# Early score masks by ScalarE and GpSimd, r loads from ScalarE's queue, and a denser start of the weight conversion, in a fused RWKV-7 and feed-forward kernel

## Chip, cores and metric

One core of one Trainium2 chip. The metric is device time in microseconds (us), the median over several executions of one program. All timed runs quoted here are of the fast state unless a line says otherwise. Profile times are counted from the start of the profiled execution. PE is TensorE's matmul side and PEld its weight loads, DVE is VectorE, ACT ScalarE, POOL GpSimd, SP SyncE. A "q" behind an engine's name means its sequencer issuing DMAs.

## The reference, cut to what matters

```python
# r, k, v, w, a, b: 4 x 8 x 768 x 40 (batch, heads, time, head size), float32
for t in range(S):
    y[:, :, t] = einsum('bhd,bhde->bhe', r_t, state)
    Sa = einsum('bhde,bhe->bhd', state, a_t)
    state = state * w_t[..., None, :] - einsum('bhd,bhe->bhde', Sa, b_t)
    state = state + einsum('bhd,bhe->bhde', v_t, k_t)
x = y as 3072 x 320                  # tokens x (heads * head size)
h = x @ w_in                         # 320 -> 2048
out = (h * clip(h + 3, 0, 6) / 6) @ w_out    # 2048 -> 320
```

## The kernel before

The recurrence is computed in chunks of time. Work is cut into units (a chunk of some heads); four units make a group (`NU` = 4). Inside a chunk the recurrence becomes small matrix products, masked "score" matrices, and one triangular inversion per group on VectorE. The feed-forward part of earlier units fills TensorE. The weights arrive as 64-bit floats and are turned into float32 by VectorE and ScalarE, piece by piece, between the other work.

A score is a 64 x 64 product in PSUM. Its mask keeps one triangle. Before the change VectorE makes it, into a score tile whose other triangle is already zero:

```python
def masked(o):
    turn[0] += 1
    x = score[turn[0] % len(score)]
    for i in range(2):
        nc.vector.copy_predicated(out=x[:, 4*i:4*i+4, :], mask=mask4, data=o[i])
    return x
```

Three scores of a unit are used: E (needed before the inversion, by a product EV), K and B (both needed by y, the unit's result). B is made just ahead of y, and y's B half cannot start without it:

```python
def s_H():
    x = scores(m["UT"], m["RT"], swap=True)
    yield PE
    m["B"] = masked(x)

def s_y():
    y = ps_pair(NPR, BL)
    for name in "KB":
        ...        # matmuls with m["K"], then with m["B"]
    yield PE
    ...
    # GpSimd: yg = ys * gam; then s_move, s_move2: eight DMAs xt <- yg on the Sync queue
```

Each unit's r is fetched, four DMAs on the Sync queue, once the previous unit's r has been transposed:

```python
def s_RT():
    x = turn_pairs(o["RN"])
    yield PE
    m["RT"] = turned("RT")
    nc.scalar.activation(out=m["RT"][:], in_=x[:], func=AF.Copy)
    fetch("R", i + 1)
    ...            # GpSimd scale, VectorE scaling of the state
```

A `yield` in a stage is where other work may be put in. In the first group's round three steps of the weight conversion are put in at every such place; a step is one or two instructions, and each piece begins with a VectorE instruction that needs a raw load, also from the Sync queue:

```python
# load_weights(), one piece (each yield ends a step)
nc.vector.tensor_scalar(x, hi, 20, 0x7FF, ...)        # L265: waits for the raw load
nc.scalar.activation(out=x, in_=x, func=AF.Relu, ...) # L267
yield
nc.vector.tensor_scalar(m, hi, 0xFFFFF, ...)          # L270
nc.scalar.activation(out=m, ...)                      # L272
yield
...                                                   # L278, L280, L285; then load()

# the first group's round
for t in range(LAST + OWN):
    for i in range(NU):
        if 0 <= t - APART * i < OWN and t - APART * i != 11:
            ...
            run(chains[i], weight=3)
```

So between the score product of `s_H` and its mask stand three weight steps, in the order of VectorE's queue. In these traces VectorE and ScalarE run their instructions in the order in which the program gives them (the kernel `first` below moves three masks in the program, and just these change places in VectorE's trace); this becomes the point of the study.

## Time and profile before

| | before |
|---|---|
| median of the first 3 runs (lowest to highest) | 869.31 us (868.46 to 870.34) |
| profiled execution, granted TensorE clock | 868.8 us, 0.94 |
| busy: PE, PEld | 786.5 us (91%), 670.6 us (77%) |
| busy: DVE, ACT, POOL | 534.3, 288.7, 152.8 us |
| first group's inversion, first F transpose to closing transpose | 40.28 to 79.04 us |
| first feed-forward matmul | 122.65 us |
| W of the next group transposed | 152.54 us |
| steady feed-forward reached (twelve matmuls in a row) | 204.97 us |

The last four rows are milestones read from the timeline. They are the way to read a kernel whose tail is full: if the work of TensorE and its order do not change, the time moves only as far as the last milestone moves. A wait list has one line for each pair of waiter and releaser, with us in total, times, and the longest. A number in brackets at the end of a timeline line is the engine's idle time just ahead of that instruction, and what ended it.

### The profile page before, as it was taken

The page shows a single profiled execution, that of the slowest core. Times are in us where ns is not written, and L with a number is a line of the kernel's source. Part 1 is how long each engine was busy: PE and PEld are TensorE (multiplying, and loading weights), DVE is VectorE, ACT ScalarE, POOL GpSimd, SP SyncE. Part 2 cuts the span into 40 slices and gives each one's busy share as a digit, 9 for nine tenths or more (in the row PEclk, how much of TensorE's full clock was granted, in tenths as well). Part 3 has the DMA queues.
Part 4 walks back from the last instruction along what each step waited for, and adds up shares of the span by engine and source line. Part 5 has one row for each costly group of instructions (what it writes and reads, how often), then busy time and mean ns, then how long its engine had stood idle before and what let it go on. Part 6 is the DMA issues. An engine that isn't in the chain of part 4 may idle for free.

```text
span 868.8 us, 36251 instructions
## 1 busy us (share of the span) xinstructions
PE 786.5 (91%) x16128; PEld 670.6 (77%) x16128; DVE 534.3 (62%) x1141; ACT 288.7 (33%) x694; POOL 152.8 (18%) x295
## 2 busy tenths in 40 slices
PE   4711988798999999999999999999999999999998
PEld 4510876786888788888888888788888888888886
DVE  7999678978845579733679453787445774221211
ACT  1334644232333322533323433233342224322211
POOL 4221011122121130220221122112212202000000
PEclk9755569998999999999999999999999999999999
DMA  6533434431122231221222232121232101100000
GB/s 133 93 105 94 114 112 99 75 61 32 31 50 54 54 64 25 57 48 38 48 50 40 42 55 52 38 49 35 42 59 43 26 19 27 26 20 13 18 17 15
DMA packets 175979, 45.08 MB, mean 52 GB/s; under 512 B 157904, under 2 KB 173264, under 8 KB 175824
## 3 DMA queue, kind: packets, MB, share of 16 engines
q1 hardware_dynamic: 174768, 42.61, 24.4%
q8 instruction: 127, 2.08, 1.0%
q10 hardware_dynamic: 1056, 0.16, 0.1%
q14 instruction: 28, 0.23, 0.1%
HBM read 34.08 MB, written 3.93 MB: 44 GB/s over the span
## 4 chain that ended last, share of the span: by engine, by line
PE 71%; DVE 6%; issue 2%; ACT 1%; POOL 0%; DMA 0%; SPq 0%; DVEq 0%; ACTq 0%
PE o L830 22%; PE h L806 19%; PE any L358 5%; PE h L811 5%; PE any L376 3%; PE any L708 2%; PE any L731 2%; PE any L450 2%; DVE x L549 1%; DVE prod L543 1%; PE any L619 1%; PE any L584 1%; PE any L653 1%; PE any L572 1%; PE any L690 1%
## 5 line engine op out<-in xcount | busy, mean ns | idle before, releaser
L830 PE MATMUL o<-wout,gt 128*128 128x320 f32 x768 | 231.3, 446 | 0.5 <-issue 0.5
L806 PE MATMUL h<-xt,win 128*128 128x128 f32 x1536 | 195.9, 280 | 0.4 <-DVE gt L817 0.4
L806 PEld LDWEIGHTS h<-xt,win 128*128 128x128 f32 x1536 | 184.3, 193 | 10.1 <-DVE gt L817 0.9
L830 PEld LDWEIGHTS o<-wout,gt 128*128 128x128 f32 x768 | 139.6, 191 | 55.2 <-issue 2.0
L817 DVE SCALAR_TENSOR_TENSOR gt<-gt,h 128x512 f32<-128x512 f32 x96 | 61.5, 681 | 111.2 <-ACT gt L816 111.2
L816 ACT ACTIVATE gt<-h,three 128x512 f32<-128x512 f32 x96 | 60.8, 684 | 160.2 <-PE h L811 160.1
L741 POOL TENSOR_TENSOR yg<-ys,gam 128x512 f32<-128x512 f32 x24 | 41.4, 1725 | 219.2 <-DVE ys L738 159.9
L543 DVE TENSOR_TENSOR prod<-x 128x30 f32<-128x30 f32 (+9 forms) x180 | 63.7, 354 | 12.9 <-POOL x L534 8.1
L549 DVE TENSOR_TENSOR x<-x,prod 128x30 f32<-128x30 f32 (+9 forms) x180 | 62.6, 348 | 4.3
L473 POOL TENSOR_TENSOR KBt<-K,rgt 128x320 f32<-128x320 f32 x24 | 22.6, 941 | 221.5 <-ACT rgt L465 207.9
L811 PE MATMUL h<-xt,win 64*128 64x128 f32 x768 | 57.0, 289 | 0.0
L385 DVE COPY_PREDICATED score<-mask,any 128x256 f32<-128x256 int32 x143 | 52.9, 433 | 0.0
L811 PEld LDWEIGHTS h<-xt,win 64*128 64x128 f32 x768 | 47.7, 191 | 5.4 <-issue 0.4
L412 DVE RECIPROCAL gam<-prods 128x256 f32<-128x256 f32 x24 | 41.4, 1739 | 13.4 <-POOL yg L741 13.1
L738 DVE TENSOR_TENSOR ys<-any,ys 128x256 f32<-128x256 f32 x48 | 18.1, 418 | 45.5 <-PE any L500 29.3
L715 DVE TENSOR_TENSOR state<-any,state 128x160 f32<-128x160 f32 x48 | 13.2, 315 | 49.5 <-PE any L376 49.4
L427 DVE RECIPROCAL rgam<-prods 128x256 f32<-128x256 f32 x24 | 41.7, 1739 | 0.0
L401 DVE TENSOR_TENSOR_SCAN prods<-wm,start 128x528 f32<-128x528 f32 x24 | 30.3, 1260 | 16.4 <-ACT wm L398 14.7
L572 PE MATMUL any<-tb,F 32*32 32x32 f32 x768 | 16.0, 199 | 26.5 <-DVE tb L552 26.2
L267 ACT ACTIVATE parts<-parts,low 128x256 uint32<-128x256 uint32 x40 | 20.3, 508 | 56.1 <-DVE parts L265 55.9
L572 PEld LDWEIGHTS any<-tb,F 32*32 32x32 f32 x768 | 14.6, 115 | 29.4 <-issue 27.8
L605 ACT ACTIVATE RT<-any 128x512 f32<-128x512 f32 x24 | 14.3, 596 | 65.8 <-PE any L358 65.7
(136 smaller groups left out, 1180.1 us busy)
## 6 DMA issues: line engine op xcount, KB each, us to landing
raw<-in_moe_w_out_dram SPq DMA_DIRECT2D x20, 256.0 KB
B<-in_b_dram SPq DMA_DIRECT2D x48, 80.0 KB
K<-in_k_dram SPq DMA_DIRECT2D x48, 80.0 KB
V<-in_v_dram SPq DMA_DIRECT2D x96, 40.0 KB
R<-in_r_dram SPq DMA_DIRECT2D x96, 40.0 KB
out_dram<-ob SPq DMA_DIRECT2D x48, 80.0 KB
W<-in_w_dram SPq DMA_DIRECT2D x40, 80.0 KB
A<-in_a_dram SPq DMA_DIRECT2D x40, 80.0 KB
```

The costliest lines, as they stand in the source:

```text
L358: nc.tensor.transpose(out=o[:, n, :], in_=x[:, 2 * n:2 * n + 2, :].rearrange("p s e -> p (s e)"), identity=ident[:])
L385: nc.vector.copy_predicated(out=x[:, 4 * i:4 * i + 4, :], mask=mask4, data=o[i])
L412: nc.vector.reciprocal(gv[:, :, 0:HB], o["prods"][:, :, 0, 1:HB + 1][:, :, ::-1])
L427: nc.vector.reciprocal(rv[:, :, HB:BL], o["prods"][:, :, 1, 1:HB + 1])
L543: nc.vector.tensor_tensor(out=pv, in0=_ap(x[:], (i + 1) * L + i, [[L, n], [0, i]]), in1=_ap(x[:], i * L, [[0, n], [1, i]]), op=ALU.mult,)
L549: nc.vector.tensor_tensor(out=rest, in0=rest, in1=pv, op=ALU.add)
L741: nc.gpsimd.tensor_tensor(out=yg[:], in0=m["ys"][:].rearrange("p r q t -> p r (q t)"), in1=o["G"][:], op=ALU.mult)
L806: nc.tensor.matmul(out=hp[c][:, i, :], lhsT=win[:, t, j * P:(j + 1) * P], rhs=xt[:, t, :], start=(t == 0 and i == 0), stop=False)
L811: nc.tensor.matmul(out=hp[c][:, i, :], lhsT=win2[half(c), (j0 + i) * P:(j0 + i + 1) * P], rhs=xt[half(c), 2, :], start=False, stop=(i == N ...
L816: nc.scalar.activation(out=gt[:], in_=hp[c][:], func=AF.Relu, bias=three[:], scale=1.0)
L817: nc.vector.scalar_tensor_tensor(out=gt[:], in0=gt[:], scalar=6.0, in1=hp[c][:], op0=ALU.min, op1=ALU.mult)
L830: nc.tensor.matmul(out=op[:], lhsT=gts[c][:, n, :], rhs=wout[:, c * HJ + r * NQ + n, :], start=((split or r == 0) and c == 0 and n == 0), ...
```

## The change

The intent is to take work off VectorE in the stretch where it is full. The masks E of units 0 to 7, and K and B of units 0 to 3, become two ScalarE copies out of PSUM and two GpSimd selections. The r of units 1 to 3 is issued by ScalarE, so that the Sync queue is free for raw weights. At the round's first step twelve weight steps and not three are put in at each place.

```diff
-    def masked(o):
+    def masked(o, early):
         turn[0] += 1
         x = score[turn[0] % len(score)]
+        if early:
+            for i in range(2):
+                nc.scalar.activation(out=x[:, 4*i:4*i+4, :], in_=o[i], func=AF.Copy)
+            for q in range(2):
+                nc.gpsimd.affine_select(
+                    out=x[half(q)], in_=x[half(q)], pattern=[[0, H], [1, BL]],
+                    compare_op=ALU.is_gt, fill=0.0, base=0, channel_multiplier=-1)
+            return x
         ...
-            o["E"] = masked(x)
+            o["E"] = masked(x, i < 2 * NU)
-            fetch("R", i + 1)
+            fetch("R", i + 1, nc.scalar if i < NU - 1 else nc.sync)
-            m["K"] = masked(x)
+            m["K"] = masked(x, i < NU)
-            m["B"] = masked(x)
+            m["B"] = masked(x, i < NU)
-                run(chains[i], weight=3)
+                run(chains[i], weight=3 if t else 12)
```

More of the change, by code (lines that the diff above doesn't have):

```diff
@@ L379, in scores @@
         return o
-    def masked(o):
+    def masked(o, early):
         turn[0] += 1
         x = score[turn[0] % len(score)]
+        if early:
+            for i in range(2):
+                nc.scalar.activation(out=x[:, 4 * i:4 * i + 4, :], in_=o[i], func=AF.Copy)
+            for q in range(2):
[3 more added lines that the diff above has]
+            return x
         for i in range(2):
```

## The prediction

> **What bounds the kernel now.** I read the page's busy slices first, then busy time by stretch, then who waited for whom on TensorE, then single stretches of the timeline. In the slices each digit is tenths of a slice of 21.7 us.
>
> ```profile
> PE   4711988798999999999999999999999999999998
> DVE  7999678978845579733679453787445774221211
> PEclk9755569998999999999999999999999999999999
> ```
>
> TensorE is full from about the tenth slice to the end; before that there is one hole (slices three and four) in which VectorE is full, and the granted clock is about half for a while. The table of stretches gives the sizes (stretch; its length; busy time and count of PE, PEld, DVE, ACT, POOL; clock; DMA share; GB/s):
>
> ```profile
> 44.00:81.00 37.00, 2.76 (x64) 2.52 (x64) 36.74 (x126) 12.82 (x34) 5.57 (x8) 0.50 0.38 104
> 86.40:122.60 36.20, 33.66 (x836) 29.34 (x837) 25.88 (x85) 21.79 (x53) 2.50 (x5) 0.55 0.39 108
> 122.60:161.00 38.40, 30.96 (x704) 25.86 (x706) 30.92 (x78) 16.55 (x44) 6.79 (x15) 0.91 0.41 97
> 206.00:868.80 662.80, 652.69 (x13131) 555.79 (x13130) 363.04 (x735) 207.78 (x486) 106.61 (x194) 0.99 0.20 38
> ```
>
> From 206 us on TensorE is busy 652.7 of 662.8 us. The change leaves TensorE's instructions and their order as they are (I compared the built orders: none of its rows moves), so that tail is a constant, and the time is "when does TensorE reach that point". Before it there are two regimes. From 44 to 81 us VectorE is busy 36.7 of 37 us: it runs the inversion of the first group, interleaved with weight conversion, and TensorE waits 26.2 us for its end. From 86 to 122 us TensorE itself is busy 33.7 of 36.2 us at a clock of 0.55: there VectorE, at 25.9 us, is not the bound. What TensorE waited for between 81 and 206 us, apart from that one wait (us, times, longest):
>
> ```profile
> PE any L358 <- DMA R<-in_r_dram: 3.4, 1, 3.4
> PE any L674 <- ACT U L658: 3.0, 2, 2.2
> PE any L500 <- issue: 2.4, 1, 2.4
> PE any L376 <- DVE state L715: 2.2, 1, 2.2
> PE any L358 <- DMA K<-in_k_dram: 2.1, 1, 2.1
> PE any L731 <- DVE score L385: 1.7, 1, 1.7
> PE any L619 <- DVE state L610: 1.6, 1, 1.6
> PE any L500 <- DVE score L385: 1.3, 1, 1.3
> ```
>
> These add to 17.7 us. They and the 44 to 81 us stretch are all that the change can work on; that is about 2% of the time, so a change beyond 2% would need nearly all of them.
>
> **What the Trainium skill says.** (1) "SBUF — State Buffer", section "Who interferes with whom": a VectorE instruction with two SBUF inputs contends with a GpSimd instruction that reads SBUF, and the one that comes second waits for the whole of the first. The trace agrees; this is the inversion beside two GpSimd products:
>
> ```profile
> 44.42 1.09 POOL L473 TENSOR_TENSOR KBt<-K,rgt 128x320 f32<-128x320 f32 x1
> 44.71 0.87 DVE L549 TENSOR_TENSOR x<-x,prod 128x30 f32<-128x30 f32 x1
> 46.80 0.21 DVE L549 TENSOR_TENSOR x<-x,prod 128x58 f32<-128x58 f32 x1
> ```
>
> The small 30-column addition took 0.87 us, one nearly twice as wide took 0.21 us when GpSimd was quiet: a loss of about 0.65 us. Later a conversion product took 1.37 us instead of 0.42 beside a 1.31 us GpSimd product. (2) "ScalarE: Activation LUTs", section "What ACT_TABLE_LOAD costs": an ACTIVATE with immediate scale and bias takes 186 ns + 0.833 ns per element, so 399 ns for 256; the trace has 382 ns for the same shape out of PSUM, and such copies start about 0.31 us apart. (3) "DMA: Bandwidth & Descriptors", section "Issuing engines are not separate DMA queues": another issuing engine saves only the sequencer's time. Here that time is large: four transfers of r hold the issuing sequencer 2.6 to 3.4 us. (4) "TensorE: Matmul & The Clock Gate", Part 1: about 3.4 us of sustained activity releases the clock. The trace agrees only in part: the clock stays near half from 86 to about 124 us though TensorE is busy, and rises some 3.5 us after the first dense feed-forward matmuls (at 122.65 us).
>
> **The change part by part.** *Masks.* E of units 0 to 7, K and B of units 0 to 3: 16 masks. Removed from VectorE: 32 predicated copies at 431 ns, 13.8 us busy; a pair occupies 0.66 us of the queue, so 10.6 us. Added: 32 ScalarE copies at some 0.31 us spacing (10 us) and 32 GpSimd selections of 64 x 512. For these the trace has only other shapes of the same operation: 128x1024 took 1.27 us undisturbed, 128x128 took 0.29. The line through both gives 0.71 us for 512 columns. Two copies of 32x1024 on disjoint partitions ran one after the other (2.13 us together), so I expect no overlap: 1.4 us per mask. A mask's own delay thus goes from 0.66 us to about 0.7 + 1.4 = 2.1 us.
>
> - Units 0 and 1, at 30.4 us: VectorE saves 1.3 us. But TensorE is full there from 30.9 to 39 us, and its EV products wait for the mask. GpSimd is busy until 30.4 us, then four selections end at about 33.2, against 31.6 now; EV, the transposes behind it and the F products come about 1.1 us later, and the inversion starts that much later: **+1.1 us**.
> - Units 2 and 3, inside the inversion: VectorE saves 4 starts of 0.33 us, 1.3 us. Four selections fall into a stream of two-input work; by the cases above a GpSimd instruction costs VectorE its duration less about 0.25 us, 4 x 0.45 = 1.8 us: **+0.5 us**.
> - K and B in the first round: VectorE saves 8 x 0.66 = 5.3 us, and 16 selections at 0.45 us, two thirds of them meeting two-input work, cost it 4.8 us. Near zero for VectorE. What remains is that masks no longer stand in VectorE's queue behind weight pieces: the waits for scores (1.7) can go. The longer way shows where y follows H closely: I take 0.4 us in each of four units, **+1.6 us**.
> - E of units 4 to 7: TensorE waits 2.4 + 1.3 us for the last two now, since the copies stand between inversion steps. GpSimd is held by four products until 200.1 us, so the new masks come at 201.5 and 203: **-0.5 us**.
>
> *r by ScalarE.* Three times four issues, 2.7 us each, leave the Sync queue and block ScalarE. The one r that TensorE waits for (3.4 us) is unit 0's, and it is not moved. The first moved one stands between RT and the two copies of tinv: ScalarE reaches tinv at 91.9 instead of 89.4 us and then VT at 94.3 instead of 92.4, and TensorE, full there, loses **+1.9 us**. The other two find idle time. In return the Sync queue is free 9 us earlier and VectorE's waits for raw weights (2.4, 2.7 and 2.5 us between 117 and 145 us) shrink.
>
> *Denser weights.* Nine more conversion steps before the first scaling of the state, some 3 us, fit into VectorE's idle 3.9 us at 86.5 to 90.4 us: free, and everything after has two pieces less to share the queue with.
>
> *Credit of the last two and the masks together.* Waits of TensorE between 110 and 161 us that trace back to a late VectorE: U 2.2 (a ScalarE step ahead of it waited for a piece held up by a GpSimd product), state 1.6, scores 1.7, S 0.9, U 0.8, and part of K's DMA (2.1), whose issue follows that chain. Sum 9.3; I take half, **-4.7 us**. Total: 1.1 + 0.5 + 1.6 - 0.5 + 1.9 - 4.7 = **-0.1 us**.
>
> **The rivals.** First, *the masks win outright*: if the selections neither lengthen VectorE's work nor delay EV, the inversion ends some 2.6 us sooner and most of the 9.3 us goes: about 858 to 860 us. For it: VectorE full at 44 to 81 us. Against: the measured collisions. Second, *a new wait takes the place*: ScalarE blocked by issues, or GpSimd's longer masks; 872 to 876 us. For it: TensorE full and ScalarE busy 21.8 of 36.2 us from 86 to 122 us. Third, *the clock*: if the first dense matmuls come some us earlier or later, the half-clock stretch shifts with them; a few us either way, already tied to the same path.
>
> **Range and chances.** The working says 869.2. Two choices of mine: taking half of 9.3 us is cautious, and the change looks fitted part to part (only early masks, only the r's that would sit behind the denser weights), which speaks for a gain that a hand sum misses. I move to **866.5 us**, 8 in 10 between 859 and 873. Faster by over 2% (below 851.9) needs all waits gone and a shorter inversion: 0.03. Slower by over 2% (above 886.7): 0.01. Within 2%: 0.96.
>
> **What would show it.** The start of the first F transpose (40.28 us) should move about 1 us later, and the transpose that ends the inversion (79.04) 1 to 2 us later; sooner by 2 us would be the first rival. Selections of about 0.7 us, and inversion steps of 0.6 to 0.9 us beside them. ScalarE's tinv copies 2 us later after its first r issue. The waits on scores in TensorE's list gone, raw-weight waits of VectorE under 3 us in sum. The stretch from TensorE's arrival in the steady part to the end unchanged at 663 us; if that moves by over 2 us, my premise of a constant tail is wrong.

## The result, and the profile after

The changed kernel is correct. Its median is **878.15 us** (876.13 to 879.28, 4 runs) against 869.83 us (868.46 to 870.44, 4 runs) for the kernel before. The ratio is 1.0095, with a 95% interval from 1.0072 to 1.0118; it is formed, here and below, as the mean time of one kernel's fast runs over that of the other's fast runs of the same rounds, so it is not quite the ratio of the medians. The change costs about 8 us: less than 2%, but above the predicted range of 859 to 873. The two profiled executions lie closer together, with spans of 868.8 and 874.4 us: the profiled one of the kernel before was timed at 870.48 us, above all four of its runs, and that of the changed kernel at 876.13, the lowest of its four.

The busy slices of the changed kernel:

```profile
PE   4710987888999999999999999999999999999998
DVE  7899777677855669834579543787545774221211
PEclk9755559999999999999999999999999999999999
```

VectorE stays full in the third and fourth slices, and has 6 and 7s in the seventh to tenth where it had 7 to 9: it is relieved, but not in the hole (the stretch of the inversion, where TensorE has almost nothing to do). TensorE has lost a tenth in the fourth, seventh and ninth slices and gained one in the eighth; the clock has lost one in the sixth (6 to 5), where the first dense matmuls now come later. What TensorE waited for between 81 and 215 us in the changed kernel (us, times, longest; the wait for the inversion and three others that hardly changed are left out):

```profile
PE any L740 <- POOL score L389: 6.2, 5, 4.1
PE any L509 <- POOL score L389: 2.7, 2, 2.3
PE any L358 <- DMA K<-in_k_dram: 2.7, 1, 2.7
PE any L628 <- ACT ys L706: 2.2, 2, 1.3
PE any L699 <- ACT score L387: 0.8, 1, 0.8
```

The wait for U has fallen from 3.0 to 0.4 us (not shown). In its place stand 6.2 us of waits for B masks, now "POOL score", in front of y (L740; it was 1.7 us on VectorE), and 2.2 us for ScalarE's ys. The milestones (both F and closing transposes are VectorE's):

| us | before | after | shift |
|---|---|---|---|
| first F transpose | 40.28 | 40.27 | 0.0 |
| closing transpose of the inversion | 79.04 | 80.44 | +1.4 |
| first feed-forward matmul | 122.65 | 127.83 | +5.2 |
| W transposes of the next group | 152.54 | 159.31 | +6.8 |
| steady feed-forward | 204.97 | 212.11 | +7.1 |
| from there to the end | 663.8 | 662.3 | -1.5 |

TensorE's count is 16128 instructions in both. Of the 7.1 us by which the steady part comes later, 1.4 arise in the inversion and 5.4 between its end and the W transposes. The clock stays at half for longer too: TensorE is granted full speed from between 126.0 and 126.5 us before, and from between 129.0 and 129.5 after. What that costs by itself was not measured.

### The profile page after: what moved, and what is told of

It is laid out like the page before. It is cut to its first block, busy times and chain, and to the rows that moved or that the text cites. A ratio compares the mean times of both kernels' runs of the same rounds, so it can differ in the third digit from the quotient of the medians.

```text
span 874.4 us, 36298 instructions
## 1 busy us (share of the span) xinstructions
PE 787.2 (90%) x16128; PEld 670.8 (77%) x16128; DVE 529.8 (61%) x1109; ACT 297.2 (34%) x726; POOL 177.1 (20%) x327
## 4 chain that ended last, share of the span: by engine, by line
PE 69%; DVE 5%; issue 3%; DMA 1%; ACT 1%; POOL 1%; SPq 0%; POOLq 0%; DVEq 0%; ACTq 0%
PE o L839 22%; PE h L815 18%; PE h L820 5%; PE any L358 5%; PE any L376 3%; PE any L717 2%; PE any L740 2%; PE any L459 2%; PE any L628 1%; PE any L593 1%; PE any L662 1%; PE any L581 1%; DVE x L558 1%; DVE prod L552 1%; PE any L699 1%
## 5 line engine op out<-in xcount | busy, mean ns | idle before, releaser
L482 POOL TENSOR_TENSOR KBt<-K,rgt 128x320 f32<-128x320 f32 x24 | 24.5, 1022 | 221.5 <-ACT rgt L474 207.8
L394 DVE COPY_PREDICATED score<-mask,any 128x256 f32<-128x256 int32 x112 | 41.3, 433 | 0.0
L267 ACT ACTIVATE parts<-parts,low 128x256 uint32<-128x256 uint32 x40 | 20.3, 508 | 49.8 <-DVE parts L265 45.6
L740 PE MATMUL any<-score,KBt 64*64 64x64 f32 x1536 | 31.1, 227 | 6.2 <-POOL score L389 6.2
```

The lines of the kernel that those rows point to most:

```text
L394: nc.vector.copy_predicated(out=x[:, 4 * i:4 * i + 4, :], mask=mask4, data=o[i])
L740: nc.tensor.matmul(out=y[q][half(s), pr, :], lhsT=o[name][half(q), h * D:h * D + SLOT], rhs=m[name][half(q), 4 * rs + 2 * s + j, :], start ...
```

## The experiments

Eighteen kernels were run in five calls; all gave correct results. The kernels of one call share the runs of the kernel before. An excess in us is the ratio less one, times 870 us. All but the two single looks had five rounds.

| kernel | median us (runs) | before | ratio [95%] | excess us |
|---|---|---|---|---|
| m_only | 876.77 (6) | 870.53 | 1.0068 [1.0052, 1.0083] | +5.9 |
| r_only | 871.49 (22) | 870.53 | 1.0013 [1.0000, 1.0026] | +1.1 |
| w_only | 872.78 (22) | 870.53 | 1.0023 [1.0011, 1.0034] | +2.0 |
| rw | 873.28 (13) | 870.53 | 1.0035 [1.0021, 1.0049] | +3.0 |
| e_early | 871.89 (22) | 870.60 | 1.0015 [1.0000, 1.0029] | +1.3 |
| e_late | 869.59 (13) | 870.60 | 0.9999 [0.9988, 1.0009] | -0.1 |
| k_only | 870.56 (21) | 870.60 | 1.0007 [0.9994, 1.0020] | +0.6 |
| b_only | 873.57 (6) | 870.60 | 1.0043 [1.0028, 1.0057] | +3.7 |
| b_not2 | 871.60 (22) | 870.64 | 1.0009 [0.9998, 1.0021] | +0.8 |
| b_dve | 873.28 (9) | 870.64 | 1.0028 [1.0011, 1.0046] | +2.4 |
| first | 868.51 (22) | 869.70 | 0.9995 [0.9982, 1.0007] | -0.4 |
| after_first | 873.28 (22) | 869.70 | 1.0035 [1.0022, 1.0048] | +3.0 |
| w_first | 872.56 (16) | 869.70 | 1.0033 [1.0021, 1.0045] | +2.9 |
| r4_late | 867.07 (10) | 870.60 | 0.9956 [0.9940, 0.9972] | -3.8 |
| first_r4 | 866.94 (22) | 870.60 | 0.9962 [0.9950, 0.9974] | -3.3 |
| after_first_r4 | 871.79 (22) | 870.60 | 1.0017 [1.0003, 1.0030] | +1.5 |

### Which part costs what

Four kernels take the parts one by one, or all but the masks:

```diff
 m_only: all masks as in the change; fetch("R", i + 1) and weight=3 as before
 r_only: only  fetch("R", i + 1, nc.scalar if i < NU - 1 else nc.sync)
 w_only: only  run(chains[i], weight=3 if t else 12)
 rw:     r_only and w_only together
```

> Only the masks are moved; r stays on the Sync queue and the weights keep their density. Theory A (the masks carry the loss: selections lock VectorE in the inversion and TensorE waits for a longer mask): 4 to 7 us slower than before, the inversion's closing transpose 1 to 2 us later than 79.0 us, TensorE waiting 5 us or more for selections. Rival B (r on ScalarE's queue carries it): within 2 us of before. Rival C (denser weights carry it): within 2 us of before.

> Only r of units 1 to 3 goes to ScalarE's queue. Theory A: 0 to 2 us slower, because four issues hold ScalarE 2.7 us and the copies of ys and tinv behind them start late, while the Sync queue gains; inversion unchanged at 79.0 us. Rival B: 4 us slower or more. Rival C: 0.

> Only nine more conversion steps at the head of the first round. Theory A: 1 us faster to 1 us slower by their own cost (VectorE's hole at 86 to 90 us takes them), but r of unit 1 then stands behind more raw loads in the Sync queue, so TensorE may wait 1 to 3 us for it: 0 to 3 us slower. Rival C: 4 us slower or more, and r not waited for.

> Everything but the masks: r on ScalarE's queue and denser weights, masks on VectorE. Theory A: within 2 us of before, so that the masks' share is the rest of the 8 us. Rival B or C: 4 us slower or more.

The single parts add to 5.9 + 1.1 + 2.0 = 9.0 us against 8.3 for the whole, and rw gives 3.0 where its parts add to 3.1. So the parts are additive within the error of some 3 us (an estimate from the intervals), and no part gains alone. The masks are two thirds of the loss. Two expectations deserve a look: rw should have stayed within 2 us and did not, and w_only has the expected time by another way than the expected one: r of unit 1 is not waited for (TensorE's list has one wait for an r, 3.0 us, that of unit 0).

### Which masks

```diff
 e_early: masked(x, i < NU) for E only            (E of units 0 to 3)
 e_late:  masked(x, NU <= i < 2 * NU) for E only  (E of units 4 to 7)
 k_only:  masked(x, i < NU) for K only
 b_only:  masked(x, i < NU) for B only
```

> Of the before kernel only the E masks of units 0 to 3 go to ScalarE and GpSimd. Theory A: the selections of units 2 and 3 (four of 0.7 us) stand against two-input work of the inversion and cost it about 0.45 us each, and what VectorE saves there is lost to a raw-weight wait; the closing transpose comes 1.5 to 2 us after 79.0 us and the whole is 1 to 2.5 us slower. Rival D (the inversion is shorter by the removed copies): closing transpose at 77 us or sooner, faster by 1 us or more.

> Only the E masks of units 4 to 7. Theory A: TensorE's waits for these two masks at about 201 and 204 us (3.6 us in sum) become waits for selections of about the same length: within 1 us of before. Rival D: those waits go, 2 to 3 us faster.

> Only the K masks of units 0 to 3. They are needed some 12 us after they are made, so their longer way is hidden. Theory A: only what selections cost VectorE beside weight conversion against what the copies saved: within 1 us of before. Rival E (the port alone carries the loss, wherever a selection runs): 1.5 us slower or more, since 8 of the 32 selections are here.

> Only the B masks of units 0 to 3, which y needs right after. Theory A: here is the largest part, TensorE waiting 4 us or more in sum for selections before y, the longest for unit 2, where the two copies stand on ScalarE behind a weight step that waits for a raw load: 2 to 4 us slower than before. Rival E: 1.5 us slower, the same as the K masks alone.

The four excesses add to 1.3 - 0.1 + 0.6 + 3.7 = 5.5 us against m_only's 5.9. B, the mask that its consumer waits for, is the costly one. The E masks of units 4 to 7 and the K masks cost nothing that these runs resolve.

### Where the B masks lose

This is the timeline of the kernel before around y of unit 2; the last line is its B half, whose K half ended at about 144.6 us:

```profile
145.14 0.29 DVE L265 TENSOR_SCALAR parts<-raw 128x256 uint32<-128x256 uint32 x1 [2.48 <-DMA raw<-in_moe_w_out_dram]
145.89 0.76 DVE L385 COPY_PREDICATED score<-mask,any 128x256 f32<-128x256 int32 x2
146.37 0.91 PE L731 MATMUL any<-score,KBt 64*64 64x64 f32 x32 [1.75 <-DVE score L385]
```

VectorE stood idle for 2.48 us ahead of a weight step whose raw load had not landed. The mask came behind that step in VectorE's queue, and y came behind the mask. VectorE had no lack of time here: it was waiting. The same place in the changed kernel:

```profile
145.87 0.51 SPq L249 DMA_DIRECT2D raw<-in_moe_w_out_dram  x1
149.27 0.29 DVE L265 TENSOR_SCALAR parts<-raw 128x256 uint32<-128x256 uint32 x1 [2.64 <-DMA raw<-in_moe_w_out_dram]
149.60 0.51 ACT L267 ACTIVATE parts<-parts,low 128x256 uint32<-128x256 uint32 x1 [3.16 <-DVE parts L265]
150.32 0.64 ACT L387 ACTIVATE score<-any 128x256 f32<-128x256 f32 x2
151.03 1.50 POOL L389 TENSOR_SCALAR_AFFINE_SELECT score<-score 64x512 f32<-64x512 f32 x2 [10.82 <-ACT score L387]
151.80 0.47 PE L740 MATMUL any<-score,KBt 64*64 64x64 f32 x2 [4.11 <-POOL score L389]
```

The mask has moved to ScalarE, but in ScalarE's queue it stands behind that piece's other half (L267), which waits for the same raw load through VectorE. So the mask did not escape the wait. It is longer on top of it: from the landing to the first matmul behind the mask it takes 151.80 - 149.27 = 2.5 us, against 146.37 - 145.14 = 1.2 us. That is 1.3 us of the 2.4 by which the wait before y grew (1.75 to 4.11). The other 1.1 us is the load itself: it landed 0.5 us after the K half of y ended before, and 1.6 us after it here (147.68 to 149.27). Two kernels test this reading:

```diff
 b_not2: masked(x, i < NU and i != 2) for B only
 b_dve:  as b_only, but in masked():
-                nc.scalar.activation(out=x[:, 4*i:4*i+4, :], in_=o[i], func=AF.Copy)
+                nc.vector.tensor_copy(x[:, 4*i:4*i+4, :], o[i])
```

> As b_only (+3.7 us), but the B mask of unit 2 stays on VectorE; units 0, 1 and 3 use ScalarE and GpSimd. Theory: most of the loss of b_only is the one wait of 4.6 us before y of unit 2, against 1.7 us before: +0.5 to +1.5 us in all, and no wait for a GpSimd score over 2 us in TensorE's list. Rival (each of the four masks costs its longer way): three quarters of the loss stays, +2.8 us.

> As b_only, but the two copies out of PSUM are made by VectorE and not by ScalarE; the selections stay on GpSimd. It tells the in-order queue of ScalarE from the length of the selections. Theory (for unit 2 the copies stood on ScalarE behind a weight step that waited for a raw load): the wait before y of unit 2 falls from 4.6 to about 3 us (1.7 as before, and 1.4 us of selections), the loss from +3.7 to +1.5 to +2.5 us. Rival (the selections are the whole of it): the loss stays at +3 us or more.

With unit 2's B alone back on VectorE the loss falls from 3.7 to 0.8 us, as the theory had it. Three of the four B masks by the long way cost 0.8 us, which is not resolved. The line for these masks in TensorE's waits, first of b_only, then of b_not2:

```profile
PE any L740 <- POOL score L389: 5.9, 5, 4.6
```

```profile
PE any L740 <- POOL score L389: 0.6, 2, 0.3
```

With the copies on VectorE (b_dve) the longest such wait is 3.2 us and the loss 2.4 us, both inside what the theory named. But the traces do not put the difference down to ScalarE's queue. The raw load's landing and the first matmul behind the mask, in b_only and then in b_dve:

```profile
147.26 0.29 DVE L265 TENSOR_SCALAR parts<-raw 128x256 uint32<-128x256 uint32 x1 [3.43 <-DMA raw<-in_moe_w_out_dram]
149.86 0.47 PE L740 MATMUL any<-score,KBt 64*64 64x64 f32 x2 [4.65 <-POOL score L389]
```

```profile
145.91 0.29 DVE L265 TENSOR_SCALAR parts<-raw 128x256 uint32<-128x256 uint32 x1 [3.23 <-DMA raw<-in_moe_w_out_dram]
148.31 0.47 PE L740 MATMUL any<-score,KBt 64*64 64x64 f32 x2 [3.19 <-POOL score L389]
```

From landing to matmul it takes 2.6 us in b_only and 2.4 in b_dve; the rest of the shorter wait is that the load landed 0.8 us after the K half ended and not 2.1. The intervals of the two times overlap as well. So ScalarE's queue as such is not shown to cost anything here: on either engine the copies come behind the same load.

### What a selection costs the inversion

Eight selections, and as a control eight memsets that only write, on a tile that is still zero, beside the inversion of the kernel before:

```diff
+            if i == NU - 1:                 # after unit 3's GpSimd products
+                zeros = state[1][:].rearrange("p a r d -> p (a r) d")
+                for _ in range(8):
 lock_sel:
+                    nc.gpsimd.affine_select(out=zeros[0:BL], in_=zeros[0:BL], ...)
 lock_set:
+                    nc.gpsimd.memset(zeros, 0.0)
```

> The kernel before and eight idle GpSimd selections of 64 x 512, on a tile that is zero anyway, inside the inversion. One look: the number is the time between the start of the first F transpose (40.28 us before) and the start of the transpose that ends the inversion (79.04 before), 38.76 us before. Theory (a selection reads SBUF and holds up VectorE by its 0.71 us less about 0.25): 8 x 0.45, the stretch grows by 3.6 us to about 42.4. Rival (the inversion grew for another reason, the raw load alone): 38.8, no change.

> Control of lock_sel: at the same place eight GpSimd memsets of 128 x 512, which only write. If it is the reading that collides, the stretch from the first F transpose to the closing transpose stays at 38.8 us within 0.5. If any GpSimd work there costs VectorE time, it grows as with the selections, by about 3 us.

GpSimd's timeline of each, lock_sel first:

```profile
51.21 6.84 POOL L480 TENSOR_SCALAR_AFFINE_SELECT state<-state 64x512 f32<-64x512 f32 x8
```

```profile
50.83 4.72 POOL L480 MEMSET state<- 128x512 f32 x8
```

In lock_sel the first F transpose starts at 40.44 us and the closing transpose at 82.31: 41.87 us, against 38.76 before. In lock_set it is 40.28 to 78.83: 38.55. So eight selections cost VectorE 3.1 us, 0.39 each (0.45 was my figure), and eight memsets, which only write, cost nothing. That GpSimd's reads collide with VectorE and its writes do not is what the page "SBUF — State Buffer", section "Who interferes with whom", states for VectorE instructions with two SBUF inputs, and here both halves of it are measured. (These were single looks of unknown state, 874.93 and 867.52 us; the spacing inside the trace is what was asked.)

In the changed kernel four selections lie in the inversion. GpSimd's timeline there:

```profile
52.91 1.56 POOL L389 TENSOR_SCALAR_AFFINE_SELECT score<-score 64x512 f32<-64x512 f32 x2
54.86 1.57 POOL L389 TENSOR_SCALAR_AFFINE_SELECT score<-score 64x512 f32<-64x512 f32 x2 [0.40 <-ACT score L387]
```

and VectorE's, of which some lines are left out:

```profile
53.01 0.69 DVE L265 TENSOR_SCALAR parts<-raw 128x256 uint32<-128x256 uint32 x1 [1.60 <-DMA raw<-in_moe_w_in_dram]
...
53.87 0.75 DVE L270 TENSOR_SCALAR parts<-raw 128x256 uint32<-128x256 uint32 x1
...
55.12 0.79 DVE L558 TENSOR_TENSOR x<-x,prod 128x184 f32<-128x184 f32 x1
55.83 0.87 DVE L280 SCALAR_TENSOR_TENSOR parts<-raw,parts 128x256 uint32<-128x256 uint32 x1
```

The same steps in the kernel before:

```profile
52.72 0.29 DVE L265 TENSOR_SCALAR parts<-raw 128x256 uint32<-128x256 uint32 x1
...
53.83 0.28 DVE L270 TENSOR_SCALAR parts<-raw 128x256 uint32<-128x256 uint32 x1
...
54.63 0.34 DVE L549 TENSOR_TENSOR x<-x,prod 128x184 f32<-128x184 f32 x1
54.89 0.41 DVE L280 SCALAR_TENSOR_TENSOR parts<-raw,parts 128x256 uint32<-128x256 uint32 x1
```

Four steps are longer by 0.40 to 0.47 us, 1.78 us together, one for each selection. Two of them, L265 and L270, read one tensor only, so the rule for two inputs is not the whole of it. The masks that VectorE no longer makes save some 2.0 us here (it reaches the place 1.32 us earlier, and one pair of 0.67 us lies behind it), but 1.60 us of this goes into the wait for the next raw load. 1.78 + 1.60 - 2.0 is the 1.4 us by which the inversion ends later. In e_early, where only E masks are moved, the inversion takes the same 40.17 us (40.97 to 81.14) as in the changed kernel (40.27 to 80.44).

### Taking the mask out from behind the load

If that place in the queue is the cause, then putting the B mask ahead of the three weight steps should mend it. The steps are not dropped; they follow at the next place. In the kernel before, this swaps a mask with three weight instructions at three places of VectorE's queue, and leaves the order of every other engine as it was:

```diff
     def s_H():
         x = scores(m["UT"], m["RT"], swap=True)
+        hold.append(i < NU)
         yield PE
     ...
     def run(stage, steps=0, weight=0, mixed=0):
         for at in stage:
             ...
             aside(steps, mixed)
-            for _ in range(weight):
+            debt[0] += weight
+            if hold and hold.pop():
+                continue
+            while debt[0]:
+                debt[0] -= 1
                 next(weights, None)
 first:       this, on the kernel before
 w_first:     this, on w_only
 after_first: this, on the changed kernel
```

> The kernel before, with one thing swapped: in the stage that makes the B mask of units 0 to 3, the mask is put ahead of the three weight steps that stood ahead of it in VectorE's queue, and these follow at the next stage. Nothing else moves. Theory (the wait before y of unit 2, 1.7 us, is a weight step waiting for its raw load, with the mask behind it): the wait for the score in TensorE's list falls below 0.5 us, and the time falls by 1 to 1.7 us (ratio 0.998 to 0.999). Rival (the late load then holds the next VectorE step, and TensorE waits for that): the wait turns up under another name, the time stays within 0.5 us.

> The denser weights alone, with the same swap. Theory: their loss of 2.0 us is the 4.9 us wait before y of unit 2, which is a mask behind a raw load that lands 4.9 us after VectorE came to it; with the mask ahead of it the loss is gone (ratio 0.999 to 1.0005). Rival (denser weights also hold up the rest of the chain): the loss stays at 1.5 us or more.

> The changed kernel with the same swap: the B masks' ScalarE copies and selections come ahead of the weight steps. Theory: y of unit 2 no longer waits for a raw load; its wait of 4.1 us falls to what copies and selections take, 2 to 2.3 us, and the loss of the whole change against before falls from 8.3 to about 6 us (ratio 1.007). Rival (wait moves on): the loss stays near 8 us.

The changed kernel's loss falls from 8.3 to 3.0 us, by more than I expected; the wait before y of unit 2 is gone from its list altogether. For the kernel before, the wait of 1.7 us is gone too, but S now waits 1.2 us behind the same load (at 147.75 us), and the gain of 0.4 us is not resolved. For the denser weights my theory fell: w_first is no better than w_only (+2.9 and +2.0 us, intervals overlapping). In TensorE's list w_only has this:

```profile
PE any L740 <- DVE score L394: 4.9, 1, 4.9
```

and w_first, in its place, this:

```profile
PE any L376 <- ACT S L652: 3.1, 2, 2.6
...
PE any L376 <- DVE ys L748: 1.1, 1, 1.1
```

The load still lands late (VectorE idles 3.49 us for it), and what stands behind it next is wanted as urgently. The rival, that the load holds up the rest of the chain too, was right there.

### Why the load is late

The Sync queue's timeline in the kernel before, just ahead of that load:

```profile
135.74 3.14 SPq L341 DMA_DIRECT2D R<-in_r_dram  x4
138.93 2.50 SPq L760 DMA_DIRECT2D xt<-yg  x4
141.53 2.19 SPq L249 DMA_DIRECT2D raw<-in_moe_w_out_dram  x3
```

The raw load was issued at 141.53 at the earliest (the line has three) and landed by 145.14. Ahead of it stand the moves of y and the four issues of an r, 3.14 us; it is the r of unit 4, whose turn does not come before 205 us. The change sends the r of units 1, 2 and 3 by ScalarE, and leaves this one. Denser weights do not bring the load forward either: in w_only it is issued at 145.32, behind the same r (4.10 us) and the same moves (3.47). Three kernels move this r:

```diff
-            fetch("R", i + 1)
+            if i != NU - 1:
+                fetch("R", i + 1)
     ...
         if t in (LAST + 7, LAST + 8):
             ...
             fetch(name, NU + 1)
+        if t == LAST + 8:
+            fetch("R", NU)
 r4_late:        this, on the kernel before
 first_r4:       this, on first
 after_first_r4: this, on after_first
```

> The kernel before, with the four issues of r of unit 4 moved to after K of unit 5 on the same Sync queue; nothing else moves. In the kernel before these four (3.1 us) stand just ahead of the raw load that unit 2's y ends up waiting for, and unit 4 is not wanted before 205 us. Theory (the raw load is late because the Sync queue is, not because its buffer is): the load lands about 3 us earlier, VectorE's wait for it (2.5 us) and TensorE's wait before y (1.7 us) fall below 0.5 us, and the time falls by 1 to 2.5 us (ratio 0.997 to 0.999). Rival (the load waits for its buffer or for the moves of y ahead of it): landing moves by under 1 us, no change.

> r4_late together with the swap of first. If both act on the same wait they do not add: about as r4_late alone (ratio 0.997 to 0.999), and TensorE's waits for S and ys behind the load, to which the wait moved in first (1.5 and 1.0 us), shrink below 1 us together. Rival (they add, or the wait for S has another cause): S and ys stay as in first.

> The changed kernel with the mask ahead of the weight steps and r of unit 4 out of the way. Theory: what is left of the loss in after_first (+3.0 us) by the raw load (waits for S and ys of 0.7 and 1.1 us behind it) goes, +1 to +2 us is left, for r on ScalarE's queue and the 1.4 us longer inversion (ratio 1.001 to 1.0025). Rival: stays at 1.0035.

r4_late is **3.8 us faster than the kernel before** (interval of the ratio 0.9940 to 0.9972), more than I expected, and the steady point comes at 201.99 us, not 204.97. Its Sync queue:

```profile
135.21 3.09 SPq L761 DMA_DIRECT2D xt<-yg  x4
138.74 3.63 SPq L249 DMA_DIRECT2D raw<-in_moe_w_out_dram  x3
```

The issue of the raw loads begins 2.8 us earlier. VectorE's waits for raw loads of w_out between 115 and 155 us, in the kernel before and then in r4_late:

```profile
DVE parts L265 <- DMA raw<-in_moe_w_out_dram: 5.2, 2, 2.7
```

```profile
DVE parts L265 <- DMA raw<-in_moe_w_out_dram: 2.4, 1, 2.4
```

One of the two waits is gone, and from TensorE's list so are the wait before y (1.7 us) and the one for K's load (2.1 us), which is issued behind the same chain; that of U falls from 3.0 to 2.3. These three sum to more than the 3.8 us gained. The buffer was not the reason; the order of the queue was. The swap adds nothing to this (first_r4, 0.9962); that fits both acting on the same wait, though the swap alone had gained nothing that is resolved. One expectation missed: S and ys do not fall below 1 us together in first_r4 but stand at 0.9 and 0.8; none of it is behind this load, for the S wait is at 128 us and the ys waits at 109 and 128. after_first_r4 gave 1.0017, inside what was stated.

r4_late and first_r4 are the fastest kernels of the study and not told apart. With the swap and the moved r on both sides, the change still costs 1.0017 against 0.9962, about 4.8 us; with the swap alone on both sides 1.0035 against 0.9995, about 3.5 us.

### r on ScalarE's queue

ScalarE's timeline of the changed kernel at its second r, with the matmul that waited:

```profile
101.37 2.51 ACTq L341 DMA_DIRECT2D R<-in_r_dram  x3
103.93 0.42 ACT L272 ACTIVATE parts<-parts 128x256 f32<-128x256 f32 x1 [1.97 <-DMA R<-in_r_dram]
104.25 0.64 ACT L706 ACTIVATE ys<-any 128x256 f32<-128x256 f32 x2
104.67 0.98 PE L628 MATMUL any<-state,at 40*64 40x40 f32 x27 [0.84 <-ACT ys L706]
```

ScalarE does nothing for 1.97 us while its sequencer issues, and a copy that TensorE needs comes behind. The first r, which I feared most, held nothing up: from RT to the tinv copies it is 1.96 us (89.79 to 91.75) against 1.84 before (87.56 to 89.40). The whole part costs 1.1 us, barely above what five rounds resolve. VectorE's waits for raw weights do shrink in r_only as predicted (from 8.0 to 6.0 us between 81 and 206 us), but not the one that counts: y of unit 2 waits 2.8 us for its mask, 1.7 before.

## Why the prediction was wrong

**The step that failed is the credit** of 4.7 us: half of 9.3 us of TensorE's waits "that trace back to a late VectorE", which the parts were to win together. The runs show nothing of it in the time. No part alone is faster (-0.1 to +3.7 us), and the whole costs 8.3 us where its parts add to 9.0, the same within the error. Two things were wrong in the step.

First, the lateness was for the most part (5.6 of the 9.3 us) no shortage of VectorE's time that fewer masks would ease. Ahead of the scores (1.7 us) and of S (0.9) VectorE was idle, 2.48 and 2.68 us, for a raw load. Ahead of U (2.2 and 0.8) stood a weight step of 1.37 and 1.36 us, 0.42 and 0.28 elsewhere, beside GpSimd's product of y. Work taken off an engine that will wait for a load only lengthens that wait, as the 1.60 us in the inversion shows.

Second, a wait that shrinks is not time won. In the changed kernel the waits for U fell from 3.0 to 0.4 us and that for S went, so part of the credit is there in the list; but the waits before y rose from 1.7 to 6.2 us, and 2.2 us for ys were new. What does pay is shown by r4_late: an earlier load on that chain gained 3.8 us.

Step by step, predicted and then measured:

- **E of units 0 and 1** (+1.1 us): not seen. The first F transpose started at 40.27 against 40.28 us; in e_early it is at 40.97, but in b_only, which leaves E alone, at 40.68 too.
- **E of units 2 and 3** (+0.5): the selection's 0.71 us was right (708 ns in the trace), and so was its cost to VectorE (0.45 said, 0.39 measured). Of the saving, 1.60 us went into the raw load's wait. The inversion took 1.4 us longer, so the two E terms together (+1.6) came to +1.3 in e_early, with the wrong division.
- **K and B** (+1.6): mis-sized. I gave each of four units 0.4 us; k_only cost 0.6 and b_only 3.7 us, of which 2.9 in the one unit whose mask stands behind the late load. That the waits on scores would go was wrong.
- **E of units 4 to 7** (-0.5): -0.1, within the error.
- **r by ScalarE** (+1.9): +1.1, and at the second r, not the first.
- **Denser weights** (0): +2.0. The later waits did not go: the load before y of unit 2 still comes behind r of unit 4 in the Sync queue (issued at 145.32, 141.53 before), and VectorE waits 4.89 us for it where it was 2.48. No run moved that r with the denser weights alone.
- **Constant tail** (663 us): it held, 662.3 against 663.8.
- **Raw-weight waits under 3 us in sum**: missed, 5.8 us between 40 and 206 us (8.0 before).
- **The clock** rising some 3.5 us after the first dense matmul: this fits the one trace (122.65, full speed from 126.0 to 126.5), not the changed kernel (127.83, and 129.0 to 129.5). The third rival was not tested.

Without the credit my terms add to +4.6 us; the measured single parts add to 8.6 (1.3 - 0.1 + 0.6 + 3.7 + 1.1 + 2.0). So K and B (2.7 us too small) and the denser weights (2.0) come next after the credit. The move from 869.2 to 866.5 because "the change looks fitted" had no measurement under it, and it pushed the estimate away from the true value. The ScalarE copy's 399 ns is an estimate from the page's formula; the trace's 382 ns was near it. The second rival, 872 to 876 us by a new wait in place of the old, named the right places, and its range was still too low.

What stays open: the 3.5 to 4.8 us that the change costs when the mask no longer stands behind the load. The 1.4 us longer inversion and the r on ScalarE are seen in the traces; how they and the denser weights share this time was not measured.

## What to carry to other kernels

When an engine is the last releaser of a wait, look one step further, at what that engine was doing just before: if it was idle in front of a load, try to move the load's issue before lightening the engine, which gained nothing here. Before moving an instruction to another engine's queue, check that what stands ahead of it there doesn't wait for the same thing. And look in a DMA queue for a transfer that nobody needs soon: moving four issues of 3 us in all, which stood ahead of the one that mattered, was worth 3.8 us, where the whole change gained nothing.

## What the Trainium skill lacked or had wrong

- "DMA: Bandwidth & Descriptors", section "Issuing engines are not separate DMA queues": it calls the sequencer's time to initiate a DMA usually small relative to the DMA. In these runs four issues of r took 3.1 us on the Sync queue (2.5 us for three on ScalarE's), not much less than a raw load took at most from issue to landing (3.6 us, 141.53 to 145.14), and moving them was worth 3.8 us.
- "GPSIMD Engine Reference": it does not treat selections (affine_select). 64 x 512 of float32 took 708 ns on average and 658 at the median (32 of them), and pairs on disjoint partitions ran one after the other, 1.37 to 1.75 us a pair.
- "SBUF — State Buffer", section "Who interferes with whom": nothing wrong was found; it names tensor_scalar among the instructions that can contend, as L265 and L270 did here. It speaks of an exclusive lock; how much that costs in a mixed stream it does not say. Here one selection cost VectorE's stream 0.39 us on average, less than its own length, and itself took 0.86 us (6.84 us for eight); eight memsets cost VectorE nothing.
- "TensorE: Matmul & The Clock Gate", Part 1: from 86.4 to 122.6 us the clock stayed at 0.50 to 0.55 with TensorE busy 30.7 to 33.7 of 36.2 us on small products, so the page's 3.4 us of sustained activity, taken as busy time in a profile, does not tell when it is released. Neither does the time since the first dense matmul: full speed came 3.4 to 3.9 us after it in the kernel before, 1.2 to 1.7 in the changed one.
